# Output tiles in a second PSUM bank, one weight join at another place, and the first scores head by head, in a top-k attention and ELU feed-forward kernel

## The chip, the cores and the metric

The kernel runs on one core of one Trainium2 chip. The metric is the device time of one execution in microseconds; lower is better. One execution was taken by the hardware profiler, which gives the profile and the trace that this document reads; three others were timed without it.

The core's engines are named as in the profile: PE is TensorE's matmul and PEld its weight load, DVE is VectorE, ACT is ScalarE, POOL is GpSimd, SP is SyncE, which here only issues DMAs. PSUM is the memory that PE writes; it is used here in tiles of one bank (128 x 512 float32) or two.

## What is computed

```python
# q, k, v: (8, 8, 576, 64) float32
scores = q @ k^T / sqrt(64)                    # 576 x 576 for each batch and head
kth    = 32nd largest of each row
attn   = softmax(scores where scores >= kth, else -1e9)
x      = (attn @ v) with heads side by side    # 4608 x 512
h      = x @ w_in                              # 4608 x 2048
g      = h if h > 0 else exp(min(h, 0)) - 1    # ELU
out    = g @ w_out                             # 4608 x 512
```

The weights arrive as float64. The kernel reads them as pairs of 32-bit words and makes float32 of them on the chip: this is the "decoding" below.

## The kernel before

**Attention.** The work is cut into steps. A step is 128 queries of one pair of heads (or the 64 remaining queries of two pairs), and its scores are a tile `sc` of 128 x 2 x 576, one row of 576 per head. For each step:

- `scores` (L331) makes the products in two halves of 288 keys. Each half has both heads in one PSUM tile `scps` of two banks: head 0 lies in rows 0 to 63 of the `kq` tile, head 1 in rows 64 to 127. One copy per half (L368) brings both heads to `sc`.
- The search for the 32nd largest runs on DVE: `first_max` (L373, MAX8 of each head), then three times `next_max` (L379 MATCH_REPLACE8 of each head, L387 MAX8 of each head). The replaced rows are in a tile `wk`, of which there are two.
- POOL masks what is below the 32nd value: `mask` (L399 to L401), in the first six steps `mask_early`, where ACT (L428) and POOL (L431) do it. ACT takes the exp (L439), PE transposes (L481, L499), ACT copies the result to SBUF (L486), and `attend` (L532) multiplies by v. When a group of queries has all its heads, ACT copies the product to `xT` (L542), and `normalise` multiplies by the reciprocal of the sums on POOL (L547).

**Feed-forward.** 128-column tiles of `xT` are collected in blocks of one, two or three tiles (20 blocks, 36 tiles). A block that is normalised gives a list of pieces, `ffn_pieces` (L554): first 16 x 2 pieces of `hidden` (matmul L567 into a tile of the pool `ps_h`, tag "h", two buffers of one bank; ACT's exp L581, relu L582 and relu L583, POOL's subtraction L584 into `gT`), then for each tile of the block eight pieces of `project` (L586), two matmuls each (L591). The 16 matmuls of an output tile go to one tile of the pool `ps_o`, which has one buffer; after the last, ACT evicts it to `osb` (L600) and SP sends it to DRAM (L603). With blocks of three tiles a hidden tile holds one of the 16 groups of hidden units, with blocks of two it holds two, with blocks of one four.

The pools of PSUM are these; together they fill its eight banks:

```python
    ps_x = pool("ps_x", 2, space=PSUM)
    ps_av = pool("ps_av", 1, space=PSUM)
    ps_h = pool("ps_h", 2, space=PSUM)
    ps_o = pool("ps_o", 1, space=PSUM)
```

**Order.** All is issued from one loop over the steps, in an order written out by hand (`manual_schedule`); every engine works its instructions off in that order. `feed` takes pieces from the list first in, first out, as many as a running account of work and due times allows, and none before its weights are decoded. So pieces of two blocks are never mixed. After the loop the rest of the list follows.

**Decoding.** 32 weight tiles go through `weight_slot` (L200): slot i joins tile i - 2 (DVE L188 and L189, POOL L193), issues loads that have become possible, and splits tile i (ACT L182 and L183). Two slots come before the loop, four in each of the first steps, at the places 3, 4, 5 and 6, and five in steps 4 and 5, at the places 2 to 6. The places of a step in the loop's early branch are: 0 after `first_max`, then the first `next_max` (with place 1 inside it), 2, the second `next_max` (place 3 inside it, between the MATCH_REPLACE8 pair and the MAX8 pair), 4, the third (place 5 inside it), `mask_early`, 6. Between place 0 and place 2 ACT also gets the two exps of the step before.

**Start.** SP loads k, and ACT's queue q, of the first two head pairs; SP loads the third pair and then three loads of weights (3, 1 and 3 tiles). PE runs 16 transposes of a unit matrix into `ps_o` (`warm`), transposes the first pair's k and q, ACT copies k and DVE copies q to SBUF (L291, L292), and `scores` makes the first step's two halves: ACT copies the first half, DVE the second. Then the same for the second pair, with ACT alone. In the first five steps `warm(24)` is issued twice a step.

Of the kernel before, what the change touches and what calls it, by code (L numbers as in the profile page):

```python
# [61 lines left out]
def kernel(  # L62
# [268 lines left out]
    def scores(u, half, copy=nc.scalar.copy):  # L331
# [35 lines left out]
                product(i, u.hps[0], i, slice(0, P), 0, ks)  # L367
        copy(u.sc[:, :, ks], ps[:, :, 0:HS])  # L368

    def first_max(u):  # L370
        u.m1 = small.tile([P, 2, 8], FP32, tag="m1", name="m1", bufs=2)
        for i in range(2):
            nc.vector.max(u.m1[:, i, :], u.sc[:, i, :])  # L373
        u.wk = wkpool.tile([P, 2, S], FP32, tag="wk", name="wk")
        u.m, u.cur = u.m1, u.sc
# [178 lines left out]
    def ffn_pieces(blk):  # L554
        N = blk.n * P


        G = {1: 4, 2: 2, 3: 1}[blk.n]

        def hidden(f, part):  # L560
            if part == 0 and f % NG == 0:
                blk.gT.append(gpool.tile([P, NG, T], FP32, tag="g", name="gT"))
            if part == 0 and f % G == 0:
                blk.h = ps_h.tile([P, WN], FP32, tag="h", name="hps")
            ps = blk.h[:, 0 : G * N].rearrange("p (f n) -> p f n", f=G)
            for i in range(part * NC // 2, (part + 1) * NC // 2):
                nc.tensor.matmul(  # L567
                    ps[:, f % G, :],
                    w_in[:, i, f * P : (f + 1) * P],
                    blk.xT[:, i, 0:N],  # L570
                    start=(i == 0),
                    stop=(i == NC - 1),
                )
            if part == 0 or f % G < G - 1:
                return

            f0 = (f - G + 1) % NG
            g = blk.gT[f // NG][:, f0 : f0 + G, 0:N]
            n = fpool.tile([P, WN], FP32, tag="n", name="n", bufs=2)
            n = n[:, 0 : G * N].rearrange("p (f n) -> p f n", f=G)  # L580
            nc.scalar.activation(n, ps, AF.Exp)  # L581
            nc.scalar.activation(g, ps, AF.Relu)  # L582
            nc.scalar.activation(n, n, AF.Relu, scale=-1.0, bias=1.0)  # L583
            nc.gpsimd.tensor_tensor(g, g, n, ALU.subtract)  # L584

        def project(s, part):  # L586
            if part == 0:
                blk.o = ps_o.tile([P, dm], FP32, tag="o", name="ops")
            step = NF // 8
            for f in range(part * step, (part + 1) * step):  # L590
                nc.tensor.matmul(  # L591
                    blk.o[:],
                    blk.gT[f // NG][:, f % NG, s * P : (s + 1) * P],
                    w_out[:, f, :],
                    start=(f == 0),
                    stop=(f == NF - 1),
                )
            if part == 7:
                o = fpool.tile([P, dm], FP32, tag="osb", name="osb", bufs=1)
                nc.scalar.copy(o[:], blk.o[:])  # L600
                for g in blk.tiles[s]:
                    p0 = g.cols.start - s * P
                    nc.sync.dma_start(out[g.rows, :], o[p0 : p0 + g.ql, :])  # L603

        t = max(0.25, 0.667 * blk.n / 3)
        return [
            (
                NC / 2 * t,
                lambda f=f, part=part: hidden(f, part),
                max(f // 4 * NC + NC - 1, 17 if f < NG else 19),  # L610
                blk,
            )
            for f in range(NF)
            for part in range(2)
        ] + [
            (1.75, lambda s=s, part=part: project(s, part), NF + (part + 1) * NF // 8 - 1, blk)
            for s in range(blk.n)
            for part in range(8)
        ]

    ffn = []
    owed = [0.0]

    def feed(n, part):
# [62 lines left out]

    def decode(n, place):

        if place in ((2, 3, 4, 5, 6) if n in (4, 5) else (3, 4, 5, 6)):  # L690
            weight_slot()

    todo, turns, blocks_at, behind = {}, {}, {}, {}
# [37 lines left out]
    with tc.manual_schedule():  # L731
        load_qk(0, 0)
        nc.scalar.activation(rec[:], rec[:], AF.Copy)
        for hp in (1, 2):
            load_qk(0, hp)
        load_weights(3)
        warm(16)
        for hp in range(2):
            transpose_qk(0, hp, shared=hp == 0)
            steps[hp].kq = {hp: kqT[0, hp]}  # L740
            scores(steps[hp], 0)
            scores(steps[hp], 1, nc.vector.tensor_copy if hp == 0 else nc.scalar.copy)
            if hp == 0:
                load_qk(0, 3)
        load_weights()
        load_v(0, 0)
        first_max(steps[0])
        weight_slot()
        weight_slot()
        for hp in range(2):  # L750
            keep_kq(0, hp)
        for n in range(NS + 4):
            early = n < EARLY
            now, last, done = (
                steps[n + d] if 0 <= n + d < NS else None for d in (0, -1, -2)
            )
            for fn, args in todo.pop(n, []):
                fn(*args)
            gone = None
            if early:  # L760
                if n + 2 < NHP:
                    transpose_qk(0, n + 2)
                ahead = steps[n + 2]
                ahead.kq = {hp: kqT[0, hp] for hp in ahead.hps}
                for half in range(2):
                    scores(ahead, half)
                if n < EARLY - 1:
                    warm(24)
            elif n % 2 == 0:

                for d in (2, 3):
                    if n + d < NS:
                        for half in range(2):
                            scores(steps[n + d], half)
                    if d == 2:
                        for u in steps[n - 4 : n - 2]:
                            if not u.attended:
                                attend(u)
                                gone = u
                for u in steps[n + 4 : n + 6]:  # L780
                    load_kq(u)
                for fn, args in behind.pop(n, []):
                    fn(*args)
            if n in turns and not early:
                transpose_qk(*turns[n])
                load_next()
            if now and n > 0:
                first_max(now)
            if last and n > EARLY:
                biases(last, early)  # L790
                mask(last, 0)
            if early:
                decode(n, 0)
                feed(n, 0.5)
                if last:
                    exp(last, 0)
                    exp(last, 1)
                next_max(now, (n, 1))
                decode(n, 2)
                if last:  # L800
                    trans(last)
                feed(n, 0.5)
                next_max(now, (n, 3), last)
                decode(n, 4)
                if last:
                    attend(last)
                if n in turns:
                    transpose_qk(*turns[n])
                if n < EARLY - 1:
                    warm(24)  # L810
                next_max(now, (n, 5))
                tile_ends = last and last.ends
                mask_early(now, (lambda: normalise(last.g)) if tile_ends else None)
                decode(n, 6)
                if n >= NHP - 2:
                    load_next()
                continue
            decode(n, 0)
            feed(n, (0.3, 0.7)[n % 2])
            if now:  # L820
                next_max(now, (n, 1))
            decode(n, 2)
            if last:
                if n > EARLY:
                    mask(last, 1)
                exp(last, 0)
            if done and done.n in by_blocks:
                trans_blocks(done)
            elif done and not done.turned:
                trans(done)  # L830
            if now:
                next_max(now, (n, 3))
            decode(n, 4)
            if gone and gone.ends:
                normalise(gone.g)
            feed(n, (0.3, 0.7)[n % 2])
            if now:
                next_max(now, (n, 5))
            decode(n, 6)
            if last:  # L840
                exp(last, 1)
            if done and done.ends and not done.summed:
                sums(done)
            if n in blocks_at:
                transpose_blocks(*blocks_at[n])
        while ffn:
            ffn.pop(0)[1]()
# [33 lines left out]
```

## Time and profile before

| what | value |
|---|---|
| median of the three timed runs | 1623.85 us (1623.75 to 1624.57) |
| time of the profiled execution | 1623.01 us |
| its span, first to last instruction | 1621.2 us |
| mean granted PE clock | 0.991 |
| busy: PE, DVE, POOL, ACT | 1560.3, 1474.9, 1141.6, 905.5 us |
| first MAX8 on DVE | at 11.15 us |
| last instruction but one on DVE (L451) | at 1540.53 us |
| last output tile: last matmul ends, eviction | 1617.41, 1617.44 to 1618.03 us |

How to read it. Times in the trace count from the span's start. In the timeline a row has the start, the length, the engine, the line of the kernel, the operation with the tile written and the tiles read, the shape, the number of instructions merged in the row, and in brackets the idle time of the engine before it with what ended it. A float32 matmul shows as two records; their ends are modelled, and records of a series overlap. A row of the view of waits has who waited for whom, the sum in us, the number of times and the longest. In the view of busy time by stretch, a row has the stretch, its length and the busy time of PE, PEld, DVE, ACT and POOL with the number of instructions, then the granted clock, the busy share of the DMA engines and GB/s.

### The profile page before, as it was taken

How to read it: one execution, taken by the hardware profiler on the slowest of the kernel's cores; microseconds unless marked ns; L12 is line 12 of the kernel's file. 1: busy time of each engine (PE TensorE's matmuls, PEld its weight loads, DVE VectorE, ACT ScalarE, POOL GpSimd, SP SyncE). 2: the span in 40 equal slices, each digit the busy share in tenths (PEclk: the TensorE clock that was granted, in tenths of full speed). 3: DMA queues.
4: the chain of work that ended last, by engine and by line, in shares of the span. 5: the costliest groups of instructions: out<-in, count | busy, mean ns of one | idle time of the engine just before them, and what ended most of it. 6: DMA issues, size and time to landing. Idle time of an engine off the chain costs nothing.

```text
span 1621.2 us, 28833 instructions
## 1 busy us (share of the span) xinstructions
PE 1560.3 (96%) x9948; PEld 1066.8 (66%) x9948; DVE 1474.9 (91%) x3070; ACT 905.5 (56%) x1857; POOL 1141.6 (70%) x1448
## 2 busy tenths in 40 slices
PE   7878999999999999999999999999999999999999
PEld 5765778777675858676565665565565585757665
DVE  7999999999999999999999999989999999899700
ACT  6875666555564756565574575465475364545321
POOL 3777777777786878778687687678677676767621
PEclk8989999999999999999999999999999999999999
DMA  9773454442121413232423524333332552453300
GB/s 311 246 219 120 147 180 141 131 129 104 42 111 51 152 58 117 72 94 82 119 71 104 183 80 116 108 102 103 109 113 76 151 161 96 121 135 89 87 13 14
DMA packets 226706, 188.70 MB, mean 116 GB/s; under 512 B 180480, under 2 KB 188672, under 8 KB 226560
## 3 DMA queue, kind: packets, MB, share of 16 engines
q1 hardware_dynamic: 224192, 186.26, 38.1%
q8 instruction: 79, 1.29, 0.3%
q10 hardware_dynamic: 2368, 0.59, 0.2%
q14 instruction: 67, 0.55, 0.1%
HBM read 151.26 MB, written 35.54 MB: 115 GB/s over the span
## 4 chain that ended last, share of the span: by engine, by line
PE 80%; DVE 8%; POOL 5%; ACT 3%; issue 2%; DMA 1%; SPq 0%; DVEq 0%; POOLq 0%; ACTq 0%
PE ops L591 27%; PE hps L567 27%; PE avps L532 9%; PE scps L348 9%; PE eps L481 6%; DVE m L387 3%; DVE wk L379 3%; POOL sc L401 1%; POOL gT L584 1%; POOL wk L399 1%; POOL wk L400 1%; PE eps L499 1%; DVE raw L189 1%; PE qkps L299 0%; DVE m L373 0%
## 5 line engine op out<-in xcount | busy, mean ns | idle before, releaser
L387 DVE MAX8 m<-wk 128x8 f32<-128x576 f32 x864 | 609.8, 748 | 0.0
L567 PE MATMUL hps<-xT,w_in 128*128 128x256 f32 (+2 forms) x2560 | 531.8, 363 | 13.5 <-POOL xT L547 9.1
L591 PE MATMUL ops<-w_out,gT 128*128 128x512 f32 x1152 | 518.8, 596 | 7.5 <-ACT osb L600 7.5
L567 PEld LDWEIGHTS hps<-xT,w_in 128*128 128x128 f32 x2560 | 406.5, 193 | 118.8 <-issue 19.7
L379 DVE MATCH_REPLACE8 wk<-m,wk 128x576 f32<-128x576 f32 x576 | 423.6, 743 | 0.0
L401 POOL TENSOR_TENSOR sc<-sc,wk 128x576 f32<-128x576 f32 x276 | 389.4, 1411 | 23.1
L591 PEld LDWEIGHTS ops<-w_out,gT 128*128 128x128 f32 x1152 | 210.1, 190 | 244.4 <-issue 219.1
L439 ACT ACTIVATE sc<-sc,neg 128x576 f32<-128x576 f32 x288 | 224.1, 779 | 215.0 <-POOL sc L401 210.6
L584 POOL TENSOR_TENSOR gT<-gT,n 128x512 f32<-128x512 f32 (+1 forms) x160 | 186.4, 1169 | 178.7 <-ACT n L583 175.9
L368 ACT COPY sc<-scps 128x576 f32<-128x576 f32 x287 | 169.3, 641 | 118.3 <-PE scps L348 115.4
L399 POOL TENSOR_SCALAR wk<-sc,nth 128x576 f32<-128x576 f32 x276 | 207.1, 750 | 26.9
L379 DVE MATCH_REPLACE8 wk<-m,sc 128x576 f32<-128x576 f32 x288 | 211.8, 744 | 0.0
L373 DVE MAX8 m<-sc 128x8 f32<-128x576 f32 x288 | 201.0, 740 | 0.1
L348 PE MATMUL scps<-kq 64*128 64x288 f32 (+3 forms) x1344 | 181.5, 419 | 20.2 <-ACT sc L368 10.9
L400 POOL TENSOR_SCALAR wk<-wk 128x576 f32<-128x576 f32 x276 | 184.3, 668 | 22.9
L532 PE MATMUL avps<-et,vE 128*64 128x128 f32 (+1 forms) x3200 | 176.7, 266 | 6.0 <-ACT et L486 3.6
L532 PEld LDWEIGHTS avps<-et,vE 128*64 128x64 f32 x3200 | 158.9, 137 | 31.9 <-issue 23.7
L486 ACT COPY et<-eps 128x1024 f32<-128x1024 f32 x132 | 132.7, 1005 | 68.9 <-PE eps L481 67.6
L581 ACT ACTIVATE n<-hps 128x512 f32<-128x512 f32 (+1 forms) x160 | 88.9, 556 | 134.8 <-PE hps L567 132.0
L348 PEld LDWEIGHTS scps<-kq 64*128 64x128 f32 (+1 forms) x1344 | 101.9, 175 | 88.7 <-issue 32.6
L481 PEld LDWEIGHTS eps<-ident,sc 128*128 128x128 f32 x1056 | 122.1, 141 | 49.2 <-issue 31.9
L481 PE MATMUL eps<-ident,sc 128*128 128x128 f32 x1056 | 138.1, 273 | 6.4 <-ACT sc L439 3.4
(74 smaller groups left out, 957.4 us busy)
## 6 DMA issues: line engine op xcount, KB each, us to landing
kq<-kqd SPq DMA_DIRECT2D x152, 576.0 KB
kqd<-kq SPq DMA_DIRECT2D x32, 576.0 KB
rb<-recd SPq DMA_DIRECT2D x64, 128.0 KB
out_dram<-osb SPq DMA_DIRECT2D x32, 256.0 KB
ed<-sc SPq DMA_DIRECT2D x12, 576.0 KB
et<-ed SPq DMA_DIRECT2D x48, 144.0 KB
kin<-in_k_dram SPq DMA_DIRECT2D x18, 256.0 KB
qin<-in_q_dram SPq DMA_DIRECT2D x17, 256.0 KB
```

What stands on the lines that cost most here:

```text
L348: nc.tensor.matmul(ps[rows, j, at : at + keys.stop - keys.start], u.kq[hp][r, 1, q0 : q0 + g.ql], u.kq[hp][r, 0, keys], start=True, stop=True,
L373: nc.vector.max(u.m1[:, i, :], u.sc[:, i, :])
L379: nc.vector.match_replace(u.wk[:, i, :], u.m[:, i, :], u.cur[:, i, :], TAKEN)
L387: nc.vector.max(u.m[:, i, :], u.cur[:, i, :])
L399: nc.gpsimd.tensor_scalar(pen, s, u.nth[:, i : i + 1], 2.0**100, ALU.add, ALU.mult)
L401: nc.gpsimd.tensor_tensor(s, s, pen, ALU.add)
L439: nc.scalar.activation(s, s, AF.Exp, bias=u.neg[:, i : i + 1], scale=scale, accum_out=g.den[:, at : at + 1],)
L481: nc.tensor.transpose(ps[:, i, c * P : (c + 1) * P], e[:, k0 + c * P : k0 + (c + 1) * P], ident[:],)
L532: nc.tensor.matmul(g.av[r, hp, 0:ql], vE[g.b, hp][:, i, (c + i) % (J + 1), :], u.et[:, at, q0 : q0 + ql], start=(c == 0), stop=(c == J),)
L567: nc.tensor.matmul(ps[:, f % G, :], w_in[:, i, f * P : (f + 1) * P], blk.xT[:, i, 0:N], start=(i == 0), stop=(i == NC - 1),)
L584: nc.gpsimd.tensor_tensor(g, g, n, ALU.subtract)
L591: nc.tensor.matmul(blk.o[:], blk.gT[f // NG][:, f % NG, s * P : (s + 1) * P], w_out[:, f, :], start=(f == 0), stop=(f == NF - 1),)
```

## The change

There are three edits; pools, tiles and arithmetic stay as they are.

1. Output tiles are counted. Every second one (number 1, 3, 5 and so on) goes to a tile of `ps_h`, tag "h", in place of the one of `ps_o`. It takes its turn in the two buffers of the hidden tiles.
2. In steps 4 and 5 the slot of place 2 moves to place 0, right behind `first_max`.
3. The first step's scores are made by a function of their own, head by head: the two halves of head 0 in one PSUM tile with one copy by ACT, then head 1. Nine more transposes of the unit matrix go ahead of them. Of the three loads of weights, the first goes ahead of the loads of the third head pair.

```diff
+    def scores_by_head(u):
+        u.sc = scpool.tile([P, 2, S], FP32, tag="sc", name="sc")
+        hp = u.hps[0]
+        for i in range(2):
+            ps = ps_x.tile([P, 2, JP], FP32, tag="x", name="scps")
+            r = slice(i * D, (i + 1) * D)
+            for half in range(2):
+                nc.tensor.matmul(
+                    ps[:, half, 0:HS],
+                    u.kq[hp][r, 1, u.g.qt * P : u.g.qt * P + u.g.ql],
+                    u.kq[hp][r, 0, half * HS : (half + 1) * HS],
+                    start=True,
+                    stop=True,
+                )
+            nc.scalar.copy(
+                u.sc[:, i, :].rearrange("p (n k) -> p n k", n=2), ps[:, :, 0:HS]
+            )
...
         def project(s, part):
             if part == 0:
-                blk.o = ps_o.tile([P, dm], FP32, tag="o", name="ops")
+                blk.o = (
+                    ps_h.tile([P, WN], FP32, tag="h", name="ops")
+                    if next(tile_count) % 2
+                    else ps_o.tile([P, dm], FP32, tag="o", name="ops")
+                )
...
     ffn = []
+    tile_count = iter(range(B * S // P))
...
-        if place in ((2, 3, 4, 5, 6) if n in (4, 5) else (3, 4, 5, 6)):
+        if place in ((0, 3, 4, 5, 6) if n in (4, 5) else (3, 4, 5, 6)):
             weight_slot()
...
-        for hp in (1, 2):
-            load_qk(0, hp)
-        load_weights(3)
+        load_qk(0, 1)
+        load_weights(1)
+        load_qk(0, 2)
+        load_weights(2)
         warm(16)
         for hp in range(2):
             transpose_qk(0, hp, shared=hp == 0)
             steps[hp].kq = {hp: kqT[0, hp]}
-            scores(steps[hp], 0)
-            scores(steps[hp], 1, nc.vector.tensor_copy if hp == 0 else nc.scalar.copy)
             if hp == 0:
+                warm(9)
+                scores_by_head(steps[0])
                 load_qk(0, 3)
+            else:
+                for half in range(2):
+                    scores(steps[hp], half)
```

## The prediction

> **What bounds the kernel now.** I read the page's chain first, then the busy time by stage, then TensorE's own waits, and last the timeline at the places that the diff touches.
>
> ```profile
> PE 80%; DVE 8%; POOL 5%; ACT 3%; issue 2%; DMA 1%; SPq 0%; DVEq 0%; POOLq 0%; ACTq 0%
> L591 PE MATMUL ops<-w_out,gT 128*128 128x512 f32 x1152 | 518.8, 596 | 7.5 <-ACT osb L600 7.5
> ...
> 160.00:792.00 632.00, 623.90 (x4459) 453.89 (x4457) 620.74 (x1313) 371.85 (x755) 480.03 (x616) 1.00 0.33 106
> 792.00:1540.00 748.00, 736.61 (x4250) 465.58 (x4251) 705.04 (x1457) 404.15 (x863) 542.84 (x694) 1.00 0.40 113
> 1540.00:1621.00 81.00, 76.73 (x354) 50.48 (x352) 0.41 (x2) 19.91 (x39) 14.52 (x12) 1.00 0.04 14
> ```
>
> The first two lines are the page's (chain by engine; the costliest PE group that waits for ACT), the other three the busy time by stage: length, then PE, PEld, DVE, ACT, POOL. The chain is four fifths TensorE, and TensorE is busy 623.90 of 632.00 us, then 736.61 of 748.00. After 1540 VectorE has two instructions left and only TensorE works. So from 160 us on a stall removed from TensorE should come off the end, unless VectorE, second at 620.74 and 705.04, is what TensorE meets next. Before 160 us it is the other way round: from 11.15 us VectorE has no gap but two of 0.7 and 0.6 us, and the chain there runs over its lines.
>
> TensorE's waits after 792 us name what the diff attacks:
>
> ```profile
> PE ops L591 <- ACT osb L600: 6.2, 9, 0.7
> PE hps L567 <- ACT gT L582: 4.4, 4, 1.6
> PE hps L567 <- POOL xT L547: 3.5, 1, 3.5
> ```
>
> Nine times it waits 0.7 us for the eviction of an output tile (L600). Between 160 and 792 us there are two more, 1.4 us. These are the eleven places where a block's next output tile follows its last with no other work between.
>
> **Part 1, the second bank.** One of the nine, in the timeline:
>
> ```profile
> 1572.82 1.88 PE L591 MATMUL ops<-w_out,gT 128*128 128x512 f32 x4
> ...
> 1574.74 0.59 ACT L600 COPY osb<-ops 128x512 f32<-128x512 f32 x1 [12.07 <-PE ops L591]
> ...
> 1575.38 1.98 PE L591 MATMUL ops<-w_out,gT 128*128 128x512 f32 x4 [0.68 <-ACT osb L600]
> ```
>
> Four records take 1.88 us, the last of them 0.59, so records start every (1.88 - 0.59)/3 = 0.43 us. The next tile could start at 1572.82 + 4 x 0.43 = 1574.54; it starts at 1575.38. One stall costs 0.84 us, more than the idle 0.68, because the array's pipeline also drains. With alternate banks the next tile need not wait for L600 at all. Nine after 792 us: 9 x 0.84 = 7.6 us.
>
> Are they kept? TensorE's other waits after 792 (4.4 us on gT) are loops that TensorE itself starts (hps to ACT, to POOL's gT and mask, to ACT's relu), so they move with it. VectorE waits 41.6 us in 25 places after 160 us, all for POOL's mask (sc L401), which stands behind gT L584 in POOL's queue; an earlier TensorE lets these shrink. I keep all nine.
>
> The two stalls before 792 (502.18 and 677.09) meet a stretch in which VectorE leads: the chain from 716.81 to 784 us is its lines, and TensorE then idles 3.47 us for xT (792.74). What VectorE can make up there is its own gaps behind POOL after 502 us: 0.52 at 569.59 and 0.91 at 716.81, 1.4 us of the 1.7. I take 1.4; ends 0 and 1.7.
>
> What the new bank adds: a block's first output tile in "h" takes the buffer of the last hidden tile but one, and waits until ACT's relu (L582) has read it. Fourteen first tiles have odd numbers. In this trace that relu ends 2.06 to 8.29 us before the block's first L591 (eight of the fourteen between 2.0 and 3.2). So it costs nothing; if that cover goes, see the second rival. After a block that ends in "h" (tiles 1, 3, 5, 17, 23) the second hidden tile needs the eviction, 0.59 us, with at least four matmuls of the first hidden tile before it: nothing.
>
> **Part 2, the first scores.**
>
> ```profile
> 7.94 2.29 PE L348 MATMUL scps<-kq 64*128 64x288 f32 x8 [1.14 <-DVE kq L292]
> 9.32 0.64 ACT L368 COPY sc<-scps 128x576 f32<-128x576 f32 x1 [2.04 <-PE scps L348]
> 10.28 0.76 DVE L368 COPY sc<-scps 128x576 f32<-128x576 f32 x1 [2.26 <-PE scps L348]
> 11.15 1.42 DVE L373 MAX8 m<-sc 128x8 f32<-128x576 f32 x2
> ```
>
> The granted clock is 0.50 from 7.96 to 11.37 us: TensorE had worked only 1.9 of the 3.4 us before. At full clock the same eight records take 1.24 us (12.92). The nine added transposes take 9 x 0.11 = 1.0 us (24 of them take 2.84 us at 31.21) and fill 6.80 to 7.9, inside the wait for the kq copies. The heads now come one after the other: the two matmuls of head 0 lie on the same 64 rows, four records 0.24 us apart, about 1.15 us to the last result. Then ACT's copy (0.64) and 0.1 to the search: 7.94 + 1.2 + 0.64 + 0.1 = 9.9 instead of 11.15, 1.25 us earlier; ACT copies head 1 while VectorE searches head 0. At half clock head 0 takes 2.3 us and head 1's copy comes late: between 0.2 earlier and 0.4 later.
> In the Trainium skill, TensorE: Matmul & The Clock Gate (What's actually happening) says the clock follows windows of 3413 ns that run free of the kernel's start. The trace agrees on the length (4.54, 7.96, 11.37); by the rule the phase may differ in another run, but with the nine transposes no window from 5.4 us on is idle, so the sum by it is the same.
>
> What becomes of the 1.25 us? Weights must come earlier too. ACT splits the first at 15.23, 0.33 us after idling for its transfer, and that load now goes ahead of the third step's k and q: 1.5 MB at the 381 to 422 GB/s of 11 to 18 us, from about 7 us on, there at about 12. That works. But the transfers are one saturated stream (share 0.9 or more in every microsecond from 3 to 30), the reorder adds no byte and removes none, and the first attention product (L532, 37.23 and 37.76) waits for v from it. From there 24 transposes, scores (43.38), exp, transposes and ACT's split (49.43 to 50.73) follow rigidly, and VectorE's L189 at 50.98 needs that split: 0.25 us of slack. So I keep 0.2 us of 1.25; ends 1.25 earlier, 0.4 later.
>
> **Part 3, the join moved from place 2 to place 0** in steps 4 and 5: on VectorE two instructions (0.41 and 0.68 us) go ahead of the first MATCH_REPLACE pair; on ACT two (0.68 each) ahead of both exps. No instruction is added, the order on POOL and SP stays, and PE's too. Step 4 now:
>
> ```profile
> 69.19 2.80 POOL L431 TENSOR_TENSOR sc<-sc,wk 128x576 f32<-128x576 f32 x2 [0.56 <-ACT wk L428]
> 71.94 1.48 POOL L193 TENSOR_TENSOR w_in<-w_in,w_out 128x512 uint32<-128x512 uint32 x1
> ...
> 71.78 0.50 DVE L188 TENSOR_SCALAR w_out<-w_out 128x512 uint32<-128x512 uint32 x1
> 72.20 1.78 DVE L189 SCALAR_TENSOR_TENSOR raw<-raw 128x512 uint32<-128x512 uint32 x1
> ```
>
> L189 takes 1.78 instead of 0.68 and ends 0.56 after POOL's L193 has: VectorE stood still meanwhile. In step 5 both do (1.12 and 1.79) beside L431 and L193. At place 0 this collision goes, but L188 would start at 69.00 and L189 at 69.34, just as POOL's L431 asks at 69.19. If POOL goes first, as in the row, L189 ends at 69.34 + 1.40 + 0.56 = 71.3: 2.3 us for the join, against 2.2 now. In step 5 it meets L547 (84.64 to 85.91) and then L431: 3.05 against 2.75. So I take 0.4 us lost for both. Ends: both collisions gone, 1.1 + 1.8 = 2.9 gained; or L189 waits out both halves of L431 each time, 1.7 lost per step, 3.4. ACT's exps come 1.3 us later there; TensorE, which needs them, idles in these steps anyway (7.53 us before the scores at 105.35).
> In the Trainium skill, SBUF — State Buffer (Who interferes with whom) has this as a lock: a VectorE instruction with two SBUF inputs, or in a two-port mode, excludes a GpSimd instruction that reads SBUF, and the loser waits for the whole of it. It speaks against this part: by the rule the move only exchanges partners, and the sum is the one above; without it, by the uncontended 0.41 and 0.68, the move would gain 2.9 us.
>
> **Sum.** -7.6 - 1.4 - 0.2 + 0.4 = -8.8 us. The profiled execution took 1623.01 us (span 1621.2), which gives 1614.2; the median shown is 0.84 higher, 1623.85, and the forecast for a median is **1615.0**. Its own ends: 1623.85 - 7.6 - 1.7 - 1.25 - 2.9 = 1610.4, and with bare gaps (9 x 0.69 = 6.2), nothing before 792, 0.4 and 3.4 lost, 1621.5.
>
> **Rivals.**
> 1. *The start loses.* The stalls go, but the joins wait out both L431 (3.4) and the clock stays half (0.4): 1623.85 - 9.0 + 3.8 = 1618.7. For: every join beside a POOL operation here was held. Against: L188 did get in between two POOL operations at 88.67.
> 2. *The h bank stalls; slower.* If ACT reads hidden tiles d us later than now, the fourteen first tiles wait the sum of (d - slack). It equals the gain at d = 3.5 us and is 13.0 at d = 4: 1615.0 + 13.0 = 1628.0. For: ACT waits up to 7.2 us for POOL's sc. Against: those waits stand in the slacks already, and ACT's queue gets no new work.
> 3. *VectorE is the bound and the change does not pay.* TensorE then waits for masks instead; only the stalls after VectorE's last gap (1489.71) count, 1509.78 and 1575.38: 1.7 us, 1622.2. For: VectorE is at 94 to 98%. Against: its 41.6 us of waits for POOL.
>
> **Chances.** Forecast 0.74, rival 1 0.12, rival 2 0.07, rival 3 0.07. Faster by over 0.2% (3.25 us, about what a measurement of this kernel can tell from no change) means below 1620.6: 0.85, the forecast and rival 1 less 0.01 for the forecast's slow end; within 0.2% 0.08; slower 0.07. The range 1610.5 to 1621.5 takes in the forecast's ends and rival 1 and leaves out rivals 2 and 3, 0.14.
>
> **What would show it.** Right: no wait of ops for osb left; next tiles 0.43 us after the last record; the first MAX8 at 9.9 and clock 1.00 there; L189 of step 4 held by L431; about 1.4 us won by 792 and 7.6 from there on. Wrong: TensorE waits for gT L582 or exp growing by as much as osb's went, or first tiles of a block waiting for L582.

## The result, and the profile after

The changed kernel takes **1612.9 us** (median of four runs, 1611.64 to 1616.43), the kernel before 1624.21 beside it: a ratio of 0.9933, with a 95% interval of 0.9918 to 0.9947, or 8.6 to 13.3 us less. The forecast was 1615.0 in a range of 1610.5 to 1621.5. The profiled execution took 1612.7 us (span 1610.9), where 1614.2 had been forecast for it.

Lines of the changed kernel shift: L567 is now L586 (hidden), L591 is L615 (output tile), L600 is L624 (its eviction), L532 is L551 (attend), L373 is L392 (first MAX8), L431 is L450, L547 is L566, L582 is L601. L378 and L385 are the new scores and their copy. L188, L189 and L193 stay.

The page of the changed kernel, chain by engine and the group of the output tiles:

```profile
PE 81%; DVE 8%; POOL 5%; ACT 3%; issue 2%; DMA 1%; SPq 0%; DVEq 0%; POOLq 0%; ACTq 0%
...
L615 PE MATMUL ops<-w_out,gT 128*128 128x512 f32 x1152 | 516.5, 596 | 0.0
```

The last number, the idle time ahead of the group, was 7.5 us and is 0.0. The bound is the same, TensorE with 81%. Its busy time by stage (stretch, length, then PE, PEld, DVE, ACT, POOL):

```profile
160.00:792.00 632.00, 623.85 (x4465) 454.85 (x4464) 623.00 (x1317) 371.83 (x756) 480.53 (x617) 1.00 0.34 107
792.00:1540.00 748.00, 742.91 (x4313) 474.68 (x4314) 703.31 (x1456) 409.58 (x874) 544.27 (x695) 1.00 0.41 113
1540.00:1611.00 71.00, 67.09 (x292) 42.46 (x288) 0.00 (x0) 13.96 (x26) 11.39 (x9) 1.00 0.03 12
```

From 792 to 1540 us TensorE idles 5.1 us instead of 11.4 (0.74 us of this difference is the end of the wait for xT, which has moved from 792.74 to 791.07, out of the stretch), and VectorE is done 9.4 us sooner (L470 starts at 1531.15). No wait has taken the old one's place: this is all that is left of TensorE's waits from 792 to 1600 us. The wait for xT just ahead of it is 3.85 us long, before 3.47.

```profile
PE hps L586 <- ACT gT L601: 4.3, 4, 1.6
PE eps L500 <- ACT sc L368: 0.8, 3, 0.3
```

The last change of tiles without other work between, in the timeline:

```profile
1559.59 12.61 PE L615 MATMUL ops<-w_out,gT 128*128 128x512 f32 x29
...
1565.37 0.58 ACT L624 COPY osb<-ops 128x512 f32<-128x512 f32 x1 [12.07 <-PE ops L615]
```

The 29 records run on without a break: (12.61 - 0.60)/28 = 0.43 us each, across the eviction at 1565.37, which before held TensorE.

**Where the time came from.** I laid TensorE's records of the two traces side by side and read how far the later one leads. The table gives the change in that stretch (minus is earlier).

| stretch | change, us | forecast | what |
|---|---|---|---|
| start to 158 us | +1.20 | +0.2 (start -0.2, joins +0.4) | VectorE is level at step 3, and 0.77 late at step 7 |
| 158 to 163 | -1.63 | not named | half clock there before, full clock now |
| 163 to 500 | +0.31 | 0 | wait before the hidden tile at 439 us |
| 500 to 780 | -1.94 | -1.4 with the next row | two stalls, 0.95 each |
| at 792 | +0.38 | | wait for xT 3.85 instead of 3.47 us |
| 800 to the end | -8.63 | -7.6 | nine stalls, 0.94 to 0.99 each |

The rows sum to -10.31, the difference of the spans is -10.3.

### The profile page after: what moved, and what is told of

It is laid out like the page before. It is cut to its first block, busy times and chain, and to the rows that moved or that the text cites. A ratio compares the mean times of both kernels' runs of the same rounds, so it can differ in the third digit from the quotient of the medians.

```text
span 1610.9 us, 28861 instructions
## 1 busy us (share of the span) xinstructions
PE 1560.2 (97%) x9957; PEld 1072.0 (67%) x9957; DVE 1474.3 (92%) x3069; ACT 905.6 (56%) x1858; POOL 1140.3 (71%) x1448
## 3 DMA queue, kind: packets, MB, share of 16 engines
q8 instruction: 79, 1.29, 0.3%
## 4 chain that ended last, share of the span: by engine, by line
PE 81%; DVE 8%; POOL 5%; ACT 3%; issue 2%; DMA 1%; SPq 0%; DVEq 0%; POOLq 0%; ACTq 0%
PE ops L615 28%; PE hps L586 27%; PE avps L551 9%; PE scps L348 9%; PE eps L500 6%; DVE m L406 3%; DVE wk L398 3%; POOL sc L420 1%; POOL gT L603 1%; POOL wk L418 1%; PE qkps L299 1%; PE idle L318 1%; POOL wk L419 1%; DMA rb<-recd 1%; PE eps L518 1%
## 5 line engine op out<-in xcount | busy, mean ns | idle before, releaser
L586 PE MATMUL hps<-xT,w_in 128*128 128x256 f32 (+2 forms) x2560 | 530.9, 363 | 14.7 <-POOL xT L566 10.4
L615 PE MATMUL ops<-w_out,gT 128*128 128x512 f32 x1152 | 516.5, 596 | 0.0
L586 PEld LDWEIGHTS hps<-xT,w_in 128*128 128x128 f32 x2560 | 406.4, 193 | 119.3 <-issue 20.0
L615 PEld LDWEIGHTS ops<-w_out,gT 128*128 128x128 f32 x1152 | 211.9, 191 | 232.9 <-issue 223.1
L392 DVE MAX8 m<-sc 128x8 f32<-128x576 f32 x288 | 200.6, 737 | 1.9 <-ACT sc L385 1.9
L348 PE MATMUL scps<-kq 64*128 64x288 f32 (+1 forms) x1336 | 179.3, 417 | 16.7 <-ACT sc L368 10.8
L551 PE MATMUL avps<-et,vE 128*64 128x128 f32 (+1 forms) x3200 | 177.7, 267 | 5.6 <-ACT et L505 3.1
L551 PEld LDWEIGHTS avps<-et,vE 128*64 128x64 f32 x3200 | 159.9, 138 | 31.5 <-issue 23.7
L600 ACT ACTIVATE n<-hps 128x512 f32<-128x512 f32 (+1 forms) x160 | 88.8, 555 | 130.8 <-PE hps L586 126.8
```

The source lines that it names most:

```text
L348: nc.tensor.matmul(ps[rows, j, at : at + keys.stop - keys.start], u.kq[hp][r, 1, q0 : q0 + g.ql], u.kq[hp][r, 0, keys], start=True, stop=True,
L551: nc.tensor.matmul(g.av[r, hp, 0:ql], vE[g.b, hp][:, i, (c + i) % (J + 1), :], u.et[:, at, q0 : q0 + ql], start=(c == 0), stop=(c == J),)
L586: nc.tensor.matmul(ps[:, f % G, :], w_in[:, i, f * P : (f + 1) * P], blk.xT[:, i, 0:N], start=(i == 0), stop=(i == NC - 1),)
L615: nc.tensor.matmul(blk.o[:], blk.gT[f // NG][:, f % NG, s * P : (s + 1) * P], w_out[:, f, :], start=(f == 0), stop=(f == NF - 1),)
```

## The experiments

Each run has a median of five runs, unless another number is given, and a ratio to the kernel before on the same chip. "Step" is a step of VectorE's search, counted from 0: step 3 is the fourth. "Late" and "earlier" are against the trace of the kernel before, unless another is named.

**1. The second bank alone** (bank_only), the kernel before with the first edit.

```diff
-                blk.o = ps_o.tile([P, dm], FP32, tag="o", name="ops")
+                blk.o = (
+                    ps_h.tile([P, WN], FP32, tag="h", name="ops")
+                    if next(tile_count) % 2
+                    else ps_o.tile([P, dm], FP32, tag="o", name="ops")
+                )
```

> The kernel before with the second bank alone. Theory: the bank is the whole gain. Each of the eleven stalls gives back 0.94 to 0.98 us (0.84 of late start and 0.10 of a slow second record), nine of them after 792 us for 8.6 us and two before it for up to 1.9 us: about 10.3 us under the kernel before, some 1613.9 us, as fast as the changed kernel or 0.5 us faster. Rival: the start and the moved join carry part of it; then this one stays 1.5 us or more behind the changed kernel, at 1614.5 us or above.

Measured: 1614.72 us (1613.5 to 1615.12), ratio 0.9944 (0.9931 to 0.9956), so 7.1 to 11.2 us less. In its trace the two early stalls give 0.95 each, and the lead grows by 8.66 from 800 to 1600 us; no wait for osb is left. The trace as a whole is 8.3 us shorter, since it is 1.13 us late at 158 us and loses 1.17 at 792. By the medians, 1614.72 against 1612.9, this is the rival's number (1614.5 or above, 1.5 behind the changed kernel). But the intervals of the two ratios overlap, the nine runs of the changed kernel have a median of 1614.46 (see 5), and the next experiment finds no gain in the other two edits. So the first edit makes the gain; that the others add a little is not excluded by this run alone.

**2. All but the second bank** (no_bank), the changed kernel with every output tile in `ps_o`.

```diff
-                blk.o = (
-                    ps_h.tile([P, WN], FP32, tag="h", name="ops")
-                    if next(tile_count) % 2
-                    else ps_o.tile([P, dm], FP32, tag="o", name="ops")
-                )
+                blk.o = ps_o.tile([P, dm], FP32, tag="o", name="ops")
```

> The changed kernel with every output tile in the old bank; the start and the moved join stay. Theory: all eleven waits of ops for osb are back at 0.7 us, VectorE is 0.8 us late from step 7 on as in the changed kernel, and the time is that of the kernel before within 1 us (1623.2 to 1625.2; which side is decided by where the half-clock windows fall). Rival: the two edits are worth 1.5 us or more together, 1622.7 us or less.

Measured: 1625.12 us (11 runs, 1621.67 to 1628.19), ratio 1.0008 (0.9999 to 1.0017): between 0.2 less and 2.8 more. The other two edits gain nothing that a measurement can tell. The eleven waits are back, nine of them after 800 us:

```profile
PE ops L611 <- ACT osb L620: 6.2, 9, 0.7
```

In this trace the two edits lose: the first search starts 1.27 us earlier, at 9.88, as forecast, and step 3 is 1.40 late, because the first attention product waits 5.7 us for v, until 39.46, and VectorE later 2.35 us for ACT's split behind it:

```profile
39.46 2.85 PE L551 MATMUL avps<-et,vE 128*64 128x128 f32 x20 [5.70 <-DMA vE<-in_v_dram]
...
51.78 0.43 DVE L188 TENSOR_SCALAR w_in<-w_in 128x512 uint32<-128x512 uint32 x1 [2.35 <-ACT w_in L182]
```

**3. The join back at place 2** (place2), the changed kernel without the move.

```diff
-        if place in ((0, 3, 4, 5, 6) if n in (4, 5) else (3, 4, 5, 6)):
+        if place in ((2, 3, 4, 5, 6) if n in (4, 5) else (3, 4, 5, 6)):
```

> The changed kernel with the slot of steps 4 and 5 back at place 2. Theory: the move only exchanges one collision with GpSimd for another; L189 is held at 72.2, 88.9 and 94.9 as before (1.78 us each), VectorE is 0.9 us earlier in step 6 than in the changed kernel, and the time is 0 to 0.9 us lower than the changed kernel's. Rival: place 0 gains what the collisions at place 2 cost; then this one is up to 2.9 us slower than the changed kernel.

Measured: 1614.44 us (1611.69 to 1616.26), ratio 0.9942 (0.993 to 0.9955); the time decides nothing. The joins are read over all traces, below 8.

**4. Without the nine transposes** (no_nine).

```diff
-                warm(9)
                 scores_by_head(steps[0])
```

> The changed kernel without the nine extra transposes of the unit matrix. Theory: they only decide the clock of the first scores; with a half-clock window there, the first head's scores take about 2.3 us in place of 1.2 and the first MAX8 comes up to 1 us later, but VectorE's wait for the split weight at the seventh join (36.7 us) shrinks by as much, and the end moves by less than 0.5 us. Rival: what the start loses goes through to the end, about 1 us slower than the changed kernel.

Measured: 1613.24 us (1610.82 to 1614.93), ratio 0.9933 (0.9921 to 0.9946). The first search starts at 10.42, step 3 at 53.73, 0.30 before that of the kernel before. What the nine transposes give is not to be seen in the time. The trace doesn't test the theory: its clock records, which begin at 6.57 us, have no half before 37.29, so the half clock that the transposes were to keep off the first scores did not come without them either.

**5. The changed kernel again** (after_again), nothing edited.

> The changed kernel once more, as the measure for the other runs of this call and for how far the clock's windows move the start from run to run. The removed stalls are worth the same wherever the windows lie: TensorE's lead over the kernel before should grow by 0.94 to 0.96 at each of the two places near 502 and 677 us and by 8.5 to 8.7 us from 800 to 1600 us. What differs from the first profile of the changed kernel should all lie before 165 us and at 792 us, up to 2 us in all. Median 1612 to 1615.

Measured: 1615.88 us (1610.66 to 1617.67), ratio 0.9943 (0.993 to 0.9957). In its trace the stalls give 0.95 each before 792 and 8.65 after 800, as expected. At 792 us it wins 1.5 where the first trace lost 0.38. The median is above what I expected. All nine runs of the changed kernel together have a median of 1614.46 and lie up to 7 us apart, those of the kernel before up to 4.3 (1621.67 to 1625.94).

**6. v loaded earlier** (v_first). In the changed kernel TensorE's first attention product waits for v:

```profile
37.43 2.89 PE L551 MATMUL avps<-et,vE 128*64 128x128 f32 x20 [2.43 <-DMA vE<-in_v_dram]
```

```diff
-        load_weights()
         load_v(0, 0)
+        load_weights()
```

> The changed kernel with the first v loaded ahead of the three weight tiles that stand in front of it in SP's queue. Theory (the start's gain was lost because the first attention product waits for v): no wait of avps for vE is left, the first attention product starts at about 36.2 instead of 37.4 us, and the fourth step's search (54.03 in the kernel before, 54.05 in the changed one) starts 0.8 to 1.3 us earlier, at 52.7 to 53.2. Of that the joins beside POOL's operations from 70 to 100 us may take up to 1, so the time is 0 to 1.2 lower than the changed kernel's. Rival (the saturated transfers are what counts, whatever their order): now the weight tiles land later, ACT's splits at 36 us or DVE's joins at 48 to 53 us wait for them, and the fourth step starts at 53.9 or later; no gain in the time.

Measured: 1612.97 us (1612.19 to 1613.48), ratio 0.9931 (0.9918 to 0.9943). The timeline of v_first at the same place:

```profile
34.89 1.38 PE L551 MATMUL avps<-et,vE 128*64 128x128 f32 x20 [0.99 <-ACT et L505]
```

The product starts 2.54 us earlier than in the changed kernel, now released by ACT, and step 3 starts at 52.91, 1.12 before that of the kernel before: nearly all of the 1.21 us by which the first search is earlier is kept. In no_bank, whose first search is as early, step 2 to step 3 takes 16.34 us, here 13.64: there v's place in the queue was the gate. It was not in the changed kernel's own trace, which takes 13.68 for it. The 0.33 us that its first search was earlier had gone before, at 36.70, where VectorE waits 0.92 us for ACT's split instead of 0.60. Nor are the waits for v all gone: the next product waits 3.06 us for its v, until 49.10. At step 7 VectorE is level again (+0.02): the joins take the 1.12 us.

**7. v earlier and the join at place 2** (v_first_p2), both edits of 3 and 6.

> As v_first, with the fifth join of steps 4 and 5 back at place 2. Theory (the move to place 0 costs 0.2 us at its own two joins and makes the next joins of step 5 collide with POOL): from the start of step 4 to the start of step 7 it loses 0.2 to 0.6 us less than v_first does, and the time is 0.2 to 0.6 lower than v_first's, the lowest of this call, 1611 to 1613. Rival (the collisions of steps 4 to 6 are decided by where each run's clock windows put DVE against POOL, not by the place): the two differ by less than 0.2 or in the other direction.

Measured: 1612.4 us (1612.08 to 1616.52), ratio 0.9938 (0.9924 to 0.9951). Step 3 leads by 1.52, step 7 is 0.65 late: from step 4 to step 7 this run loses 2.15 us where v_first loses 1.13, the other way round than the theory had it. That is the rival's outcome; its reason, the clock's windows, is not shown.

**8. POOL's join ahead of its masking** (join_first). The moved joins of the changed kernel, VectorE and POOL in the timeline:

```profile
68.98 0.41 DVE L188 TENSOR_SCALAR w_out<-w_out 128x512 uint32<-128x512 uint32 x1
69.18 3.34 POOL L450 TENSOR_TENSOR sc<-sc,wk 128x576 f32<-128x576 f32 x2 [0.56 <-ACT wk L447]
69.31 1.92 DVE L189 SCALAR_TENSOR_TENSOR raw<-raw 128x512 uint32<-128x512 uint32 x1
...
85.08 1.13 DVE L188 TENSOR_SCALAR w_out<-w_out 128x512 uint32<-128x512 uint32 x1
85.88 3.42 POOL L450 TENSOR_TENSOR sc<-sc,wk 128x576 f32<-128x576 f32 x2
86.13 1.90 DVE L189 SCALAR_TENSOR_TENSOR w_out<-w_out 128x512 uint32<-128x512 uint32 x1
...
94.34 1.28 POOL L603 TENSOR_TENSOR gT<-gT,n 128x512 f32<-128x512 f32 x1 [2.52 <-ACT n L602]
94.45 1.46 DVE L188 TENSOR_SCALAR w_out<-w_out 128x512 uint32<-128x512 uint32 x1
95.58 1.47 POOL L193 TENSOR_TENSOR w_out<-w_out,raw 128x512 uint32<-128x512 uint32 x1
95.83 1.78 DVE L189 SCALAR_TENSOR_TENSOR w_out<-w_out 128x512 uint32<-128x512 uint32 x1
```

The first two are the forecast's: L189 held by L450, the join over at 71.23 (forecast 71.3) and, from 85.08, in 2.95 us (forecast 3.05). The third was not forecast: an unmoved join of step 5 meets POOL's gT. It did so in the kernel before, too, but there gT had begun at 93.43, and L188 at 94.31 took 0.70 us.

```diff
+                if n in (3, 4):
+                    decode(n, 6)
                 mask_early(now, (lambda: normalise(last.g)) if tile_ends else None)
-                decode(n, 6)
+                if n not in (3, 4):
+                    decode(n, 6)
```

> The changed kernel with the join of place 6 issued ahead of POOL's two masking operations in the steps before the moved joins (3 and 4), so that POOL has its part of the join done before the moved join's L189 asks for the port. Theory (the moved join's L189 takes 1.9 instead of 0.68 us because POOL's masking stands beside it): L189 of the moved joins takes 0.68 to 0.9 us in step 4 or 5, and step 6 starts 1 to 2.4 us earlier against the start of step 4 than in the changed kernel (34.4 us between the two there). The masks then come 1.5 us later, and of the gain at most 1 reaches the end: the time is 0 to 1 lower. Rival (POOL's masking only moves on beside other VectorE instructions and is as long there): the total between the starts of steps 4 and 6 stays within 0.4 us, and the time is the same or up to 1 higher, because exps and TensorE's scores come later.

Measured: 1612.48 us (1611.36 to 1617.18), ratio 0.9933 (0.9921 to 0.9946). In the timeline of join_first the moved join is free, and another one is held in its place:

```profile
68.89 0.40 DVE L188 TENSOR_SCALAR w_out<-w_out 128x512 uint32<-128x512 uint32 x1
69.21 0.68 DVE L189 SCALAR_TENSOR_TENSOR raw<-raw 128x512 uint32<-128x512 uint32 x1
...
89.79 0.99 DVE L188 TENSOR_SCALAR w_out<-w_out 128x512 uint32<-128x512 uint32 x1
90.45 1.48 POOL L193 TENSOR_TENSOR w_out<-w_out 128x512 uint32<-128x512 uint32 x1
90.70 1.79 DVE L189 SCALAR_TENSOR_TENSOR raw<-raw 128x512 uint32<-128x512 uint32 x1
```

So the masking was what held the moved join. From step 4 to step 6 VectorE takes 34.05 us (kernel before 33.81, changed kernel 34.72), from step 4 to 7 it takes 48.77. The 0.67 us less than in the changed kernel lie between the theory (1 to 2.4) and the rival (within 0.4).

*The joins in all traces.* From step 4 to step 7 VectorE took 48.63 (the kernel before), 49.70, 50.02, 49.08, 49.06 and 50.78 us in the six traces with the join at place 2, mean 49.55; with the join at place 0 (leaving out the two kernels that also move POOL's join) it took 49.42, 49.41, 50.23, 50.29, 49.75 and 49.13, mean 49.71. The move costs 0.16 us within a scatter of 2. The trace that the forecast started from was the luckiest of the six.

**9. The idle stretches filled** (fill). Windows of half clock fall on other places in each trace. Of the eleven traces without this edit, seven have one after the idle stretch near 158 us; near 790 us two have none, five have one and four have two. Busy time by stretch near 158 us, the kernel before (the number after the five engines is the granted clock):

```profile
154.70:158.10 3.40, 0.56 (x6) 0.33 (x4) 3.40 (x9) 2.11 (x6) 2.11 (x2) 1.00 0.86 268
158.10:161.50 3.40, 3.40 (x16) 3.40 (x17) 3.40 (x8) 0.00 (x0) 2.32 (x5) 0.51 0.99 329
```

and the changed kernel:

```profile
157.40:160.80 3.40, 1.58 (x14) 1.58 (x15) 3.40 (x7) 1.29 (x4) 2.28 (x4) 1.00 0.98 294
160.80:164.20 3.40, 3.40 (x33) 3.40 (x32) 3.40 (x9) 1.10 (x3) 2.20 (x3) 1.00 1.05 275
```

In the first, TensorE worked 0.56 of 3.40 us and then had half the clock (16 records in the next 3.40 us); in the second the idle time is split over two windows, TensorE worked 1.58 us in the emptier one, and kept it (33 records). That is the table's -1.63.

```diff
+            if part == 0 and f == 0 and blk in (order[1], order[11]):
+                warm(18 if blk is order[1] else 28)
```

> The changed kernel with transposes of the unit matrix (as in warm) put into the two stretches in which TensorE stands idle 2.4 and 3.9 us before the first hidden tile of a block: 18 of them near 157 us, 28 near 787 us; the output stays the same. Theory (the scatter of the changed kernel, 1610.7 to 1617.7, comes from whether a window of half clock follows such an idle stretch: each costs TensorE 1.6 us; near 158 us six of ten profiles so far have one, near 790 us they have none, one or two): no record at half clock near 158 and 790 us, so the time loses 1.6 for each that a run would have had, some 2.5 us on average; median 1610 to 1612.5, scatter under 4 us. Rival 1 (what half clock costs there is taken back by waits for POOL and VectorE): the windows go but the median stays at 1613 to 1615. Rival 2 (the added transposes come out longer than the idle stretch, 18 x 0.12 = 2.1 and 28 x 0.12 = 3.3 us, or their tile waits for an eviction, and the first hidden tile starts later): up to 1 us slower than without them.

Measured: 1614.28 us (1610.97 to 1617.31), ratio 0.9941 (0.9928 to 0.9954). The windows went: the clock is 1.00 from 134 us to the end of the matmuls, and from 800 us on TensorE leads the first trace of the changed kernel by 1.7 to 1.8. But median and scatter stayed. My theory of the scatter fell. Rival 2 came true at one of the two places: near 788 us the added transposes wait for an eviction, and the hidden tile behind them starts at 791.10, 1.28 us after its xT is ready (788.53 + 1.29):

```profile
787.99 3.28 PE L318 MATMUL idle<-ident 128*128 128x128 f32 x28 [1.73 <-ACT osb L626]
...
788.53 1.29 POOL L566 TENSOR_TENSOR xT<-xT,rb 128x512 f32<-128x512 f32 x1
...
791.10 6.62 PE L588 MATMUL hps<-xT,w_in 128*128 128x384 f32 x20
```

So the edit gives back 1.3 us of what it wins there, in all three kernels that have it, and the median says little of what the windows cost.

**10. The kernel before, filled** (before_fill), the edit of 9 alone.

> The kernel before with the same added transposes at the same two places and nothing else changed. If half clock there is a cost of its own, it must go here too: 1624.1 less 1.6 near 158 us and 1.6 to 1.7 near 790 us, 1620.5 to 1622.5. If it is taken back by other waits, 1623.5 to 1625.

Measured: 1623.51 us (11 runs, 1622.25 to 1625.83), ratio 0.9999 (0.999 to 1.0008), so at most 1.6 us gained, where 1.6 to 3.3 was expected. Its trace has no half clock at either place, the hidden tile near 792 us is 1.28 us late as in fill, and TensorE leads the kernel before by 1.57 us from 800 to 1300 us. Then:

```profile
1311.93 1.21 PE L348 MATMUL scps<-kq 64*64 64x288 f32 x20
1314.76 2.40 PE L532 MATMUL avps<-et,vE 128*64 128x128 f32 x40 [1.62 <-DMA et<-ed]
```

The late steps turn their exps by a round trip through DRAM (`ed`, `et`), and an attention product waits 1.62 us for it. After that the lead is gone. In this trace the gain is turned into a new wait. That the other runs lose it in the same way is not shown.

**11. All together** (all_three), the edits of 6, 8 and 9 on the changed kernel.

> A version put together: the changed kernel with the filled idle stretches, the first v loaded ahead of three weight tiles, and the join of place 6 ahead of POOL's masking in steps 3 and 4. Theory: the start's 1.1 us are kept to step 3 (fourth search at about 52.9 us), the joins to step 7 lose 0.2 to 1.0 us of them, and the half clock near 158 and 790 us is gone: median 1609.5 to 1612, the lowest of all. Rival: what the start and the joins give is used up in VectorE's wait near 182 us, as in the changed kernel, and the time equals that of the kernel with the filled stretches alone, within 0.5.

Measured: 1611.03 us (1608.95 to 1613.36), ratio 0.9921 (0.9908 to 0.9935), the lowest of all. Its interval overlaps that of the changed kernel, so a gain over it is not shown. The trace doesn't follow the theory either: step 3 starts at 54.15, since two windows of half clock, from 12.5 and 19.4 us, took the start's gain, and step 7 is 0.86 late. The lead after 800 us is that of fill within 0.1 up to 1300; then an attention product waits 0.38 us for `et`.

**12. Only the two early stalls** (two_tiles_only), on the kernel before.

```diff
-                blk.o = ps_o.tile([P, dm], FP32, tag="o", name="ops")
+                blk.o = (
+                    ps_h.tile([P, WN], FP32, tag="h", name="ops")
+                    if next(tile_count) in (7, 11)
+                    else ps_o.tile([P, dm], FP32, tag="o", name="ops")
+                )
```

> The kernel before with only two output tiles in the other pool, numbers 7 and 11, so that just the two stalls before 792 us go (near 502 and 677) and nothing else. Theory (TensorE's lead there is kept at full length, 0.95 us each): TensorE 1.9 us ahead from 680 to 780 us, against where it stood at 500 us, and the nine later stalls as in the kernel before; time 1.4 to 1.9 below the kernel before, 1622.0 to 1622.6. Rival (VectorE leads there and the transpose chain to xT at 792 us takes it back): ahead at 780 us but not at 800 us for a like position of the clock windows, and the time within 0.5 of the kernel before.

Measured: 1623.92 us (11 runs, 1621.8 to 1624.96), ratio 0.9995 (0.9986 to 1.0004): 2.3 less to 0.6 more, which does not part the two. In the trace TensorE gains 1.90 us between 500 and 680, loses 0.12 at the wait for xT at 792, and then 1.34 to a second window of half clock, of which the kernel before has one there:

```profile
791.80:798.40 6.60, 6.03 (x10) 3.30 (x11) 6.60 (x14) 0.69 (x4) 3.74 (x6) 0.50 0.59 186
```

So VectorE does not take the two stalls back; the clock may.

## Why the prediction was right, and where it was not

- **The bound and the mechanism** held. TensorE was the bound, all eleven waits for the eviction went, the next tile starts 0.43 us after the last record, and of TensorE's other waits only the two for xT grew (by 0.31 at 439 us and 0.38 at 792). bank_only gives the gain by itself, and no_bank has the waits back and no gain.
- **The nine stalls were mis-sized**: 7.6 forecast, 8.63 measured. The term that was off is "One stall costs 0.84 us". The missing 0.10 stands in the lines that the forecast shows: four records take 1.98 us after the stall and 1.88 elsewhere, so the second record comes late as well, at 0.53 instead of 0.43. That makes 9 x 0.94 = 8.5; two of the stalls were 0.04 longer.
- **The two stalls before 792** were forecast at 1.4 of 1.7. They gave 1.9 by 680 us, and 0.38 was lost at 792: 1.56 net. What took the 0.38 is a longer wait for xT, as forecast. In the other traces that lose the two stalls and have no added transposes, that wait takes only 0.12 to 0.20, and the rest of what is lost or won at 792 (1.34 lost in two_tiles_only) goes with the clock. The number was nearly right; that VectorE's own two gaps set the loss, the reason given, is not shown.
- **The start**: "9.9 instead of 11.15" is what five of the ten traces with the new start show (9.88 in no_bank, 9.94 in v_first). In the changed kernel's own trace it was 10.82:

```profile
8.88 1.37 PE L378 MATMUL scps<-kq 64*128 64x288 f32 x8
10.14 1.18 ACT L385 COPY sc<-scps 128x576 f32<-128x576 f32 x2 [1.93 <-PE scps L378]
10.82 1.42 DVE L392 MAX8 m<-sc 128x8 f32<-128x576 f32 x2 [1.86 <-ACT sc L385]
```

  The scores take their full-clock time, but start at 8.88 instead of 7.94, since the transposes of k and q ahead of them took 1.11 and 0.96 us instead of 0.66 and 0.60. That this is half clock is read from these lengths: the clock's records in this trace begin at 7.24 us.

  Most of the 1.25 us is the clock, and not the order of the heads. With the old start the first search begins at 11.15 and 11.34 where half clock falls on the scores (the kernel before, before_fill), and at 10.24 and 10.68 where it does not (bank_only, two_tiles_only). The new start, in traces whose clock records begin within 0.1 us of those two, has 10.02 (all_three) and 10.42 (no_nine): 0.2 to 0.3 us earlier. "Clock 1.00 there" held in all nine traces with the nine transposes, but in no_nine as well, so that the transposes do it is not shown.

  That little of the gain is kept was right (0.2 forecast, 0.02 measured at step 3), but of a gain of 0.33. The gate that was named, v's landing, is the one in no_bank, as v_first shows; in the changed kernel's own trace it was ACT's split at 36.70.
- **The joins**: +0.4 forecast, +0.8 measured from step 4 to 7. At the two moved joins it is 0.02 and 0.11; the collision at 94.45 adds 0.76, set by when ACT's n comes, and step 6 gives 0.13 back. Over six traces each the move costs 0.16. Nor is it shown that the start and the joins make TensorE 1.20 late at 158 us: bank_only and two_tiles_only, which have neither edit, are 1.13 and 1.36 late there.
- **The clock**: not a term of the sum, worth 1.63 us at 158 in this pair of traces. It hid that TensorE was 1.20 late by then. Without it the profiled execution would have come out at 1614.3, beside the forecast's 1614.2: one error of the sum is the +1.0 before 158, the other the -1.0 of the nine stalls. That the two cancel is luck, and so is the clock's 1.63 in this execution.
- **The rivals**: rival 2 (the h bank stalls) and rival 3 (VectorE is the bound) have no line in any trace with the bank. Rival 1's place was right: in no_bank's trace VectorE is 3.0 us late at step 7. But 1.40 of it is v's landing, which the rival did not name, the rest comes from step 4 to step 7, where the joins are, and the half clock on the first scores did not come. In the median of the runs the loss is 1.3 (-0.2 to 2.8).

The Trainium skill, SBUF — State Buffer (Who interferes with whom), has the loser of the port wait for the whole of the other's instruction, and issue order decide who that is. The traces agree: L189 takes 1.92 us beside L450 and 0.68 where join_first moved POOL's work away, and each edit of the order only chose another loser.

What stays open is the scatter of the changed kernel, 1610.66 to 1617.67. The windows at 158 and 790 us do not set it (fill). The runs outside the profiler have no trace.

## What to carry to other kernels

An eviction stall is priced by the start of the next tile's later records, not by the idle time or the first record alone: here 0.68 idle, 0.84 to the first record, 0.94 to the second in nine of the eleven, 0.04 more in the other two. A gain on the engine that leads to the end arrives in full; one in a stretch where engines hand work to one another can be taken by the next gate (v's load, then the port, then the round trip through DRAM), and has to be followed from gate to gate. A term below some 2 us that rests on one trace ahead of a place where the clock may fall, or where POOL and VectorE meet, should carry the scatter over several traces and not that one's value.

## What the runs showed of the hardware

- The clock's windows last 3.41 us and lie at another place in every run (half clock from 158.14, 159.32, 161.74 us, or not at all). A window with little work on TensorE gives half clock to the next, 1.63 us for the series of matmuls at 158 us. How little is no fixed share. Cut into windows of 3.41 us from the first clock record on, the fourteen traces have no window at full clock with less than 1.4 us of work that was not followed by half clock, and none with more than 2.0 that was; in between both occur. 1.45 us of work in 3.40 left the clock full, in after_again near 790 us:

```profile
785.40:788.80 3.40, 1.70 (x4) 0.39 (x3) 3.40 (x8) 2.38 (x5) 3.13 (x4) 1.00 0.37 120
788.80:792.20 3.40, 1.45 (x5) 0.92 (x6) 3.40 (x8) 0.90 (x3) 1.90 (x2) 1.00 0.30 88
792.20:795.60 3.40, 3.40 (x12) 2.04 (x11) 3.40 (x8) 1.28 (x3) 2.53 (x5) 1.00 0.57 158
```

- To come back it needs more: in the same fourteen traces every window at half clock with less than 2.8 us of work was followed by another, and none with more than 2.9. In v_first it was 2.63 us:

```profile
786.40:789.80 3.40, 0.51 (x2) 0.00 (x0) 3.40 (x9) 2.74 (x6) 3.23 (x4) 1.00 0.46 151
789.80:793.20 3.40, 2.63 (x4) 1.51 (x5) 3.40 (x7) 0.39 (x2) 1.20 (x4) 0.50 0.33 95
793.20:796.60 3.40, 3.40 (x7) 1.79 (x6) 3.40 (x8) 0.51 (x2) 2.73 (x3) 0.50 0.82 275
796.60:800.00 3.40, 3.40 (x12) 2.00 (x11) 3.40 (x9) 1.76 (x5) 1.00 (x1) 1.00 0.79 177
```

- The Trainium skill, TensorE: Matmul & The Clock Gate (What's actually happening), has the windows run free of the kernel, which these traces agree with. It names an idle window as what brings the clock down. If that means a window without work, the measurement decides against it here: near 158 us in v_first a window with 1.52 us of work in 3.40 was followed by half clock.
- A transfer that a tuned order leaves just in time is a gate whose place moves: the wait for v ended at 37.2 to 37.6 us in five traces (the changed kernel, place2, no_nine, join_first, fill) and at 39.46 in no_bank, which has the same loads in the same order.
